# Splitting the loads of query and key rows, and a preparation buffer for the fourth weight's raw words, in a kernel of sparse attention and two MLPs

## The chip, the cores and the metric

The kernel runs on one core of a Trainium2 chip. The metric is the device time of one launch in microseconds (us), lower is better.

## The reference

Attention over 4 batches, 8 heads, 576 tokens and 64 elements per head is followed by two MLPs on 2304 tokens of width 512 with an inner width of 2048. The heads of the first half see the last 32 tokens, those of the second half every 32nd token before them.

```python
mask_local = (rel >= 0) & (rel < stride)
mask_strided = (rel >= 0) & (pos[None, :] % stride == pos[:, None] % stride)
scores = np.where(masks, scale * q @ k.T, -1e9);  attn = softmax(scores) @ v
h = x @ w_in;   g = s * relu(h) ** 2 + b;                     x = g @ w_out       # first MLP
h = x @ w_in;   g = where(h >= 1, h, where(h <= -1, 0, (h + 1) ** 2 / 4));  out = g @ w_out
```

The weights come as 64-bit floats.

## The kernel before

**Stages.** The tokens are cut into six units of 384. Attention is worked off in 21 tiles: three strided ones for each batch and nine local ones of 256 tokens; the text counts them in their order as tile 0, 1, 2 (strided, batch 0), 3, 4, 5 (local), 6, 7, 8 (strided, batch 1) and so on. A tile loads its rows, then PE makes scores, DVE takes the maximum (L611) and subtracts it (L628; in the first three tiles ACT's L622 does so in the exponential), ACT exponentiates (L631), DVE sums and inverts (L632 to L635), DVE or POOL normalizes (L636), PE transposes (the flip, L645), a copy brings the result to `pt` (L340 or L338), PE multiplies by the values (L661, L671), ACT copies the output to `xh` (L338) and DVE puts what the rounding lost into `xl` (L703). The first MLP (`hidden`, `output`) takes three matmuls for each product (high by high, high by low, low by high) and runs the segments unit 0, inner blocks 0 to 3; unit 1, blocks 0 to 3; unit 0, blocks 4 to 7; unit 1, blocks 4 to 7; then the other units. Unit 1 needs tiles 4 to 8. The second half of the first MLP and the whole of the second use a Strassen-like scheme with seven products, whose weights are made ahead by `prepare`, stored to DRAM from the ring `pp` (two buffers) by POOL (L401), and read back.

**Weights.** `decode` brings the words of one weight block into a buffer of the ring `raw` (three buffers, 512 KB each), ACT makes the high part of a 32-bit float (L356), DVE shifts and merges (L358, L360). `weights` splits that into a high and a low part (`w0h`, `w0l`; L338, L372). The first four blocks loaded are three of `w_ins` and one of `w_outs`; the fifth is of `w_ins` again.

**Order.** `Issue.order` is a list scheduler with costs and due times: it sets the order of all work on every engine when the program is built, and it also puts filler matmuls on the tile `warm_t` (`busy`, L576) where it expects PE to be idle in the first part. All loads go out on SP's queue in one order, save the small ones of tile 2 in batch 0, which ACT issues. The loads share eight completion semaphores (DMAHW0 to DMAHW7) in turn, so that a load is issued only when the one eight places before it has landed. `homes` names the tiles (0, 1, 3 to 7, 9, 11, 12) whose rows of queries and keys go to the space of later units' tokens (`xh5`, `xl5`, ..., printed without their number below). The two first tenants of the ring `pp` are `mask_t` and `warm_t`.

Of the kernel before, what the change touches and what calls it, by code (L numbers as in the profile page):

```python
# [12 lines left out]
I32 = mybir.dt.int32  # L13
# [6 lines left out]
DM, DFF = 512, 2048  # L20
# [10 lines left out]
KT = QT + STRIDE  # L31
# [11 lines left out]
HI_ACT, HOLD, NACC = 12, (0, 1, 3), 6  # L43
FILL, MOST, LEAST = 37.0, 5, (18.0, 2)
RAW, DT, KB, QV, SM, PT, PP, TB = 3, 2, 4, 3, 3, 2, 2, 3
BUFS = {"kb": KB, "qv": QV - 1, "qx": 1, "sm": SM - 1, "sx": 1, "pt": PT}


# [202 lines left out]
def sparse_attention_two_mlps(ctx: ExitStack, tc: tile.TileContext, loc, strd, w_ins, w_outs, fixed, out):  # L251
# [5 lines left out]
    sp = ctx.enter_context(tc.tile_pool(name="sp", bufs=2))  # L257
# [49 lines left out]
    def buf(pool, tag, shape, dtype=F32, bufs=1):  # L307
        ring = rings.setdefault((pool.name if hasattr(pool, "name") else id(pool), tag), Ring(bufs))
        ring.name = tag
        serial[0] += 1  # L310
        name = f"{tag}_{serial[0]}"
        return Buf(ring, lambda: pool.tile(shape, dtype, tag=tag, name=name, bufs=bufs))


    def act(n):
        return ("act", 0.15 + n * 0.00084, 0.1)
# [28 lines left out]
    decodes, prepared, pi_line, w_loads, w0_line, w1_line, p_line = [], [], [], [], [], [], []  # L345

    def decode(src, after=(), allocs=(), t=None, line=None, raw=None):
        raw = raw or buf(sp, "raw", [128, 2 * DM], I32, RAW)
        t = t or buf(sp, "dt", [128, DM], I32, DT)
        words = lambda i: raw.tile.rearrange("p (a b) -> p a b", b=2)[:, :, i]  # L350
        x = lambda: t.tile.bitcast(F32)
        load = op(lambda e: e.dma_start(out=raw.tile.bitcast(I64), in_=src), [dma(src.shape[0] * src.shape[1] * 8)],
                  writes=[raw], after=after, allocs=allocs, line=line)


        first = op(lambda e: e.activation(out=x(), in_=words(1).bitcast(F32), func=AF.Prelu, scale=2.0 ** -112, alpha=-2.0 ** 32),  # L356
                   [act(DM)], [raw], [t])
        op(lambda e: e.tensor_scalar(out=t.tile, in0=t.tile, scalar1=3, scalar2=None, op0=ALU.logical_shift_left),  # L358
           [dve2(DM, 0.0005)], (), [t])
        op(lambda e: e.scalar_tensor_tensor(out=t.tile, in0=words(0), scalar=29, in1=t.tile,  # L360
                                            op0=ALU.logical_shift_right, op1=ALU.bitwise_or), [dve2(DM)], [raw], [t])
        return t, x, first, load
# [84 lines left out]
    def attend(i, early):  # L447
        kind, b, d = tiles[i]
# [32 lines left out]
        QC, VC = 4 * 128, 4 * 128 + 2 * W  # L481
        if strided and d < 2:
            vb_ = room("vals")
            v4 = lambda: vb_.tile.rearrange("p (g n) -> p g n", g=2)
            if i in homes:
                both = home(homes[i][0])
                ks, qb_ = [both, both], both
                row = lambda: both.tile[:, 0:2 * VC].rearrange("p (j n) -> p j n", j=2)
                k4 = lambda j: row()[:, j, 0:QC].rearrange("p (h a n) -> p h a n", h=2, a=2)
                q4 = lambda j: row()[:, j, QC:VC].rearrange("p (h n) -> p h n", h=2)  # L490
                if i:
                    load(both, [(row, strd[b, 2 * d:2 * d + 2, :, 0:VC].rearrange("j p n -> p j n"))], 128 * 2 * VC * 4)
                else:
                    for j in range(2):
                        load(both, [(lambda j=j: row()[:, j], strd[b, 2 * d + j][:, 0:VC])], 128 * VC * 4)
            else:
                ks, qb_ = [room("wide") for _ in range(2)], room("wide")
                k4 = lambda j: ks[j].tile.rearrange("p (h a n) -> p h a n", h=2, a=2)
                q4 = lambda j: qb_.tile[:, 0:4 * W].rearrange("p (j h n) -> p j h n", j=2, h=2)[:, j]
                for j in range(2):  # L500
                    load(ks[j], [(lambda j=j: ks[j].tile, strd[b, 2 * d + j][:, 0:QC])], 128 * 2048)
                load(qb_, [(lambda: qb_.tile[:, 0:4 * W].rearrange("p (j n) -> p j n", j=2),
                            strd[b, 2 * d:2 * d + 2, :, QC:VC].rearrange("j p n -> p j n"))], 128 * 4 * W * 4)
# [37 lines left out]
        else:  # L541
            vs = [room("vals") for _ in range(2)]
            if i in homes:
                qs = ks = [home(tag) for tag in homes[i]]
                k4 = lambda pos: ks[pos].tile[:, 512:512 + 4 * KT].rearrange("p (a n) -> p a n", a=4)
                q4 = lambda pos: qs[pos].tile[:, 0:512].rearrange("p (a c n) -> p a c n", a=4, c=2)
            else:
                qs, ks = [room("wide") for _ in range(2)], [room("wide") for _ in range(2)]
# [3 lines left out]
            v4 = lambda pos: vs[pos].tile.rearrange("p (s h d) -> p s h d", s=2, h=4)  # L552
            for pos in range(2):
                if i in homes:
                    n = 512 + 4 * KT
                    load(qs[pos], [(lambda pos=pos, n=n: qs[pos].tile[:, 0:n], loc[2 * d + pos][:, 0:n])], 128 * n * 4)
                else:
                    load(qs[pos], [(lambda pos=pos: qs[pos].tile, loc[2 * d + pos][:, 0:512])], 128 * 2048)
                    load(ks[pos], [(lambda pos=pos: ks[pos].tile[:, 0:4 * KT], loc[2 * d + pos][:, 512:512 + 4 * KT])],
                         128 * 4 * KT * 4)  # L560
# [116 lines left out]
        for bank in range(2):  # L677
            cuts, bufs, n = [], [], 0
# [241 lines left out]
    n = NP  # L920
# [248 lines left out]
    for p in range(PAIRS):  # L1169
        a = len(plan.ops)  # L1170
# [118 lines left out]
```

## Time and profile before

| | us |
|---|---|
| median of 3 runs | 840.81 |
| the runs | 837.0 to 842.73 |
| the profiled execution | 843.28 |
| its span, first to last instruction | 840.7 |

PE is busy for 97% of the span, DVE for 75%, ACT for 63%, POOL for 11%; the DMA engines move 263 GB/s on average. The chain of work that ended last is 78% PE. The matmuls' ends are modelled, so a busy PE need not be one at its peak. In the first 70 us, where attention and the first weights are made, the engines wait for each other; behind that PE hardly stops.

### The profile page before, as it was taken

The page shows a single profiled execution, that of the slowest core. Times are in us where ns is not written, and L with a number is a line of the kernel's source. Part 1 is how long each engine was busy: PE and PEld are TensorE (multiplying, and loading weights), DVE is VectorE, ACT ScalarE, POOL GpSimd, SP SyncE. Part 2 cuts the span into 40 slices and gives each one's busy share as a digit, 9 for nine tenths or more (in the row PEclk, how much of TensorE's full clock was granted, in tenths as well). Part 3 has the DMA queues.
Part 4 walks back from the last instruction along what each step waited for, and adds up shares of the span by engine and source line. Part 5 has one row for each costly group of instructions (what it writes and reads, how often), then busy time and mean ns, then how long its engine had stood idle before and what let it go on. Part 6 is the DMA issues. An engine that isn't in the chain of part 4 may idle for free.

```text
span 840.7 us, 17752 instructions
## 1 busy us (share of the span) xinstructions
PE 817.7 (97%) x6308; PEld 793.1 (94%) x6312; DVE 628.7 (75%) x1333; ACT 528.3 (63%) x1122; POOL 91.5 (11%) x186
## 2 busy tenths in 40 slices
PE   7789999999999999999999999999999999999998
PEld 4579998999999999999988999999999999999998
DVE  3798638888776767878778977997576988466966
ACT  5467636565557666657576777865477854567653
POOL 1030003241221022130111000100000000000000
PEclk9999999999999999999999999999999999999999
DMA  8678285888777578899879899988987779888882
GB/s 255 215 226 287 96 259 189 288 274 275 252 264 275 184 272 277 308 315 335 296 253 319 262 372 311 331 252 268 304 255 252 253 250 283 294 253 252 249 267 95
DMA packets 107261, 221.15 MB, mean 263 GB/s; under 512 B 14118, under 2 KB 29606, under 8 KB 107174
## 3 DMA queue, kind: packets, MB, share of 16 engines
q1 hardware_dynamic: 95906, 182.89, 67.8%
q0 software_dynamic: 10240, 36.71, 11.4%
q8 instruction: 50, 0.82, 0.4%
q10 hardware_dynamic: 1028, 0.43, 0.2%
q14 instruction: 37, 0.30, 0.1%
HBM read 172.27 MB, written 47.71 MB: 262 GB/s over the span
## 4 chain that ended last, share of the span: by engine, by line
PE 78%; DMA 7%; issue 7%; DVE 5%; POOL 1%; ACT 1%; SPq 1%; ACTq 0%; POOLq 0%; DVEq 0%
PE acc L963 7%; PE acc L964 7%; PE acc L965 7%; PE h L720 6%; PE side L964 6%; PE side L963 6%; PE side L965 6%; PE h L721 6%; PE h L722 5%; PE h L964 3%; PE h L963 3%; PE h L965 3%; PE acc L720 3%; DMA dw<-pp 3%; PE acc L721 3%
## 5 line engine op out<-in xcount | busy, mean ns | idle before, releaser
L401 POOL DMA_DIRECT2D dw<-pp x80 | 54.9, 687 | 292.0 <-DVE pp L399 236.3
L720 PE MATMUL h<-xh,w0hx 128*128 128x384 f32 x192 | 65.5, 341 | 2.0 <-ACT w1hx L747 2.0
L720 PE MATMUL h<-xh,w0h 128*128 128x384 f32 x192 | 66.2, 345 | 0.8 <-issue 0.6
L721 PE MATMUL h<-xl,w0h 128*128 128x384 f32 x192 | 64.8, 337 | 0.7 <-DVE xl L703 0.7
L722 PE MATMUL h<-xh,w0lx 128*128 128x384 f32 x192 | 64.8, 338 | 0.0
L721 PE MATMUL h<-xl,w0hx 128*128 128x384 f32 x192 | 64.8, 337 | 0.0
L722 PE MATMUL h<-xh,w0l 128*128 128x384 f32 x192 | 64.6, 337 | 0.0
L747 ACT ACTIVATE t<-h 128x384 f32<-128x384 f32 x51 | 24.9, 488 | 31.0 <-PE h L722 30.8
L720 PEld LDWEIGHTS h<-xh,w0hx 128*128 128x128 f32 x192 | 36.2, 189 | 2.4 <-ACT w1hx L747 2.3
L720 PEld LDWEIGHTS h<-xh,w0h 128*128 128x128 f32 x192 | 36.3, 189 | 2.0 <-issue 0.7
L721 PEld LDWEIGHTS h<-xl,w0h 128*128 128x128 f32 x192 | 36.4, 189 | 1.0 <-DVE xl L703 1.0
L721 PEld LDWEIGHTS h<-xl,w0hx 128*128 128x128 f32 x192 | 36.3, 189 | 0.0
L722 PEld LDWEIGHTS h<-xh,w0lx 128*128 128x128 f32 x192 | 36.3, 189 | 0.0
L722 PEld LDWEIGHTS h<-xh,w0l 128*128 128x128 f32 x192 | 36.3, 189 | 0.0
L356 ACT ACTIVATE dt<-raw 128x512 f32<-128x512 f32 x42 | 27.7, 668 | 12.5 <-DMA raw<-in_w_outs 4.7
L338 ACT ACTIVATE gh<-w1h 128x384 fp32r<-128x384 f32 x48 | 24.6, 523 | 14.4 <-PE acc L965 6.3
L720 PE MATMUL acc<-gh,w1hx 128*128 128x384 f32 (+1 forms) x96 | 33.4, 348 | 0.0
L720 PE MATMUL acc<-gh,w1h 128*128 128x384 f32 (+1 forms) x96 | 33.4, 348 | 0.0
L1010 DVE TENSOR_TENSOR gl<-w1h,gh 128x384 fp32r<-128x384 f32 x48 | 26.2, 555 | 9.3 <-ACT gh L338 8.9
L399 DVE TENSOR_TENSOR pp<-dt,pp 128x512 fp32r<-128x512 f32 (+1 forms) x36 | 22.3, 619 | 14.0 <-ACT pp L338 13.9
L721 PE MATMUL acc<-gl,w1hx 128*128 128x384 f32 (+1 forms) x96 | 32.4, 338 | 0.0
L722 PE MATMUL acc<-gh,w1l 128*128 128x384 f32 (+1 forms) x96 | 32.4, 338 | 0.0
(585 smaller groups left out, 2813.0 us busy)
## 6 DMA issues: line engine op xcount, KB each, us to landing
dw<-pp POOLq DMA_DIRECT2D x60, 512.0 KB, 4.5
w0h<-dw SPq DMA_DIRECT2D x84, 256.0 KB
w0l<-dw SPq DMA_DIRECT2D x84, 256.0 KB
w0hx<-dw SPq DMA_DIRECT2D x84, 256.0 KB
w0lx<-dw SPq DMA_DIRECT2D x84, 256.0 KB
raw<-in_w_ins SPq DMA_DIRECT2D x32, 512.0 KB
raw<-in_w_outs SPq DMA_DIRECT2D x32, 512.0 KB
kb<-dw SPq DMA_DIRECT2D x56, 256.0 KB
```

The costliest lines, as they stand in the source:

```text
L338: e.activation(out=out, in_=in_, func=AF.Copy)
L356: first = op(lambda e: e.activation(out=x(), in_=words(1).bitcast(F32), func=AF.Prelu, scale=2.0 ** -112, alpha=-2.0 ** 32), [act(DM)], [r ...
L399: op(lambda e: e.tensor_tensor(out=y.tile[:, 0:nq, 1, :], in0=x(), in1=y.tile[:, 0:nq, 0, :].bitcast(F32), op=SUB), [dve2(256 * nq)], [b], ...
L401: op(lambda e: e.dma_start(out=dw[o][i][qs].rearrange("q p w n -> p q (w n)"), in_=y.tile[:, 0:nq].bitcast(F32).rearrange("p q w n -> p q ...
L720: e.matmul(out=acc, lhsT=wh, rhs=ah, start=first, stop=False)
L721: e.matmul(out=acc, lhsT=wh, rhs=al, start=False, stop=False)
L722: e.matmul(out=acc, lhsT=wl, rhs=ah, start=False, stop=last)
L747: op(lambda e: e.activation(out=c(t), in_=c(p), func=AF.Relu), [act(n)], [p], [t])
L963: e.matmul(out=dst, lhsT=wh, rhs=ah, start=opens and first, stop=False, skip_group_check=not opens)
L964: e.matmul(out=dst, lhsT=wh, rhs=al, start=False, stop=False, skip_group_check=not opens)
L965: e.matmul(out=dst, lhsT=wl, rhs=ah, start=False, stop=last, skip_group_check=not opens)
L1010: op(lambda e, g=g, hi=hi, lo=lo: e.tensor_tensor(out=lo.tile[:, 0:n], in0=g.tile, in1=hi.tile[:, 0:n].bitcast(F32), op=SUB), [dve2(n)], [ ...
```

## The change

A strided tile of `homes` after tile 0 loads its rows in four transfers (256, 126, 256 and 126 KB) in place of one of 764 KB. A local tile of `homes` loads each of its two row sets in two transfers (256 and 192 KB) in place of one of 448 KB. That is 15 and 8 transfers more. The raw words of the fourth weight block (the first of `w_outs`) go to a buffer of the ring `pp` in place of `raw`, so that the fifth block is the first that needs a `raw` buffer for the second time. The scheduler then orders everything anew.

```diff
--- before.py
+++ after.py
@@ -43,6 +43,7 @@
 HI_ACT, HOLD, NACC = 12, (0, 1, 3), 6
 FILL, MOST, LEAST = 37.0, 5, (18.0, 2)
 RAW, DT, KB, QV, SM, PT, PP, TB = 3, 2, 4, 3, 3, 2, 2, 3
+IN_PP = (3,)
 BUFS = {"kb": KB, "qv": QV - 1, "qx": 1, "sm": SM - 1, "sx": 1, "pt": PT}
 
 
@@ -345,7 +346,7 @@
     decodes, prepared, pi_line, w_loads, w0_line, w1_line, p_line = [], [], [], [], [], [], []
 
     def decode(src, after=(), allocs=(), t=None, line=None, raw=None):
-        raw = raw or buf(sp, "raw", [128, 2 * DM], I32, RAW)
+        raw = raw or (buf(sp, "pp", [128, 2 * DM], I32, PP) if len(w_loads) in IN_PP else buf(sp, "raw", [128, 2 * DM], I32, RAW))
         t = t or buf(sp, "dt", [128, DM], I32, DT)
         words = lambda i: raw.tile.rearrange("p (a b) -> p a b", b=2)[:, :, i]
         x = lambda: t.tile.bitcast(F32)
@@ -488,11 +489,9 @@
                 row = lambda: both.tile[:, 0:2 * VC].rearrange("p (j n) -> p j n", j=2)
                 k4 = lambda j: row()[:, j, 0:QC].rearrange("p (h a n) -> p h a n", h=2, a=2)
                 q4 = lambda j: row()[:, j, QC:VC].rearrange("p (h n) -> p h n", h=2)
-                if i:
-                    load(both, [(row, strd[b, 2 * d:2 * d + 2, :, 0:VC].rearrange("j p n -> p j n"))], 128 * 2 * VC * 4)
-                else:
-                    for j in range(2):
-                        load(both, [(lambda j=j: row()[:, j], strd[b, 2 * d + j][:, 0:VC])], 128 * VC * 4)
+                for j in range(2):
+                    load(both, [(lambda j=j, a=a, z=z: row()[:, j, a:z], strd[b, 2 * d + j][:, a:z])
+                                for a, z in (((0, VC),) if not i else ((0, QC), (QC, VC)))], 128 * VC * 4)
             else:
                 ks, qb_ = [room("wide") for _ in range(2)], room("wide")
                 k4 = lambda j: ks[j].tile.rearrange("p (h a n) -> p h a n", h=2, a=2)
@@ -552,8 +551,8 @@
             v4 = lambda pos: vs[pos].tile.rearrange("p (s h d) -> p s h d", s=2, h=4)
             for pos in range(2):
                 if i in homes:
-                    n = 512 + 4 * KT
-                    load(qs[pos], [(lambda pos=pos, n=n: qs[pos].tile[:, 0:n], loc[2 * d + pos][:, 0:n])], 128 * n * 4)
+                    load(qs[pos], [(lambda pos=pos, a=a, z=z: qs[pos].tile[:, a:z], loc[2 * d + pos][:, a:z])
+                                   for a, z in ((0, 512), (512, 512 + 4 * KT))], 128 * (512 + 4 * KT) * 4)
                 else:
                     load(qs[pos], [(lambda pos=pos: qs[pos].tile, loc[2 * d + pos][:, 0:512])], 128 * 2048)
                     load(ks[pos], [(lambda pos=pos: ks[pos].tile[:, 0:4 * KT], loc[2 * d + pos][:, 512:512 + 4 * KT])],
```

On SP's queue before, at the end of the loads of tiles 0 to 5: `raw` are the weights' words (0, 1, 2, 3 in order; two of `w_ins` and one of `w_outs` are seen), `xh`, `qv` and `k` belong to tile 6.

```order
L352 DMA raw_659<-in_w_ins 128x512 [waits DMAHW6_49]
L352 DMA raw_680<-in_w_ins 128x512 [waits DMAHW7_49]
L352 DMA raw_733<-in_w_outs 128x512 [waits DMAHW0_49,DMAHW1_49,DVE_49,Activation_49]
L467 DMA xh_127_746<-in_strd 128x2x764 [waits PE_49,Pool_49]
L467 DMA qv_776<-in_strd 54x2x256 [waits DMAHW2_49]
L467 DMA qv_776<-in_strd 54x2x256 [waits DMAHW3_49]
L467 DMA k_128_822<-in_strd 64x2x72 [waits DMAHW4_49,PE_49,Pool_49]
```

The same place after, and behind it the end of tile 7's loads (`xl`, `qx`) with the fifth weight (the last row).

```order
L353 DMA raw_684<-in_w_ins 128x512 [waits DMAHW7_49]
L353 DMA raw_737<-in_w_ins 128x512 [waits DMAHW0_49]
L353 DMA pp_750<-in_w_outs 128x512 [waits DMAHW1_49,DVE_49]
L468 DMA xh_127_760<-in_strd 128x512 [waits PE_49,DMAHW2_49,Activation_49,Pool_49]
L468 DMA xh_127_760<-in_strd 128x252 [waits DMAHW3_49]
```

```order
L468 DMA xl_140_862<-in_strd 128x512 [waits DMAHW5_49]
L468 DMA xl_140_862<-in_strd 128x252 [waits DMAHW6_49]
L468 DMA qx_901<-in_strd 54x2x256 [waits DMAHW7_49,PE_49]
L468 DMA qx_901<-in_strd 54x2x256 [waits DMAHW0_49]
L353 DMA raw_924<-in_w_ins 128x512 [waits DMAHW1_49,DVE_49,Activation_49]
```

The fourth weight no longer waits for ACT and for a `raw` buffer; the next wait of this kind is the fifth weight's, and ahead of it the values of tile 7 (`qx`) wait for PE.

On DVE before, around the normalization of tile 2 (`sx`, `dn_263`); `xl` rows are the outputs of tile 0.

```order
L633 TENSOR_SCALAR dn_263<-dn_263 128x8
L340 COPY pt_400<-h_399 128x512
L635 RECIPROCAL dn_263<-dn_263 128x8
L703 TENSOR_TENSOR xl_142<-side_305,xh_141 128x2x6x6
L703 TENSOR_TENSOR xl_140<-side_305,xh_139 128x2x6x12
L636 TENSOR_TENSOR sx_261<-sx_261,dn_263 128x512
L703 TENSOR_TENSOR xl_142<-side_306,xh_141 128x2x6x6
L703 TENSOR_TENSOR xl_140<-side_306,xh_139 128x2x6x12
```

POOL after, at the same place in the program: `sx` is tile 2 and `sm_352` tile 3, the copies after them are of tile 6's and tile 7's rows.

```order
L616 TENSOR_SCALAR mx_230<-mx_230 128x4
L616 TENSOR_SCALAR mx_267<-mx_267 128x4 x2
L635 TENSOR_TENSOR sx_266<-sx_266,dn_268 128x512
L635 TENSOR_TENSOR sm_352<-sm_352,dn_354 128x512
L632 TENSOR_SCALAR dn_632<-dn_632 128x8
L341 COPY k_128_839<-xh_127_760 64x2x18 x2
L341 COPY q_129_854<-xh_127_760 128x2x18
```

The normalizations of tiles 2 and 3 have moved from DVE to POOL. (On PE the values of tile 1 now stand ahead of the flip of tile 2, and the values of tile 3 ahead of the scores of tile 5.)

DVE before, from the maximum of tile 6 (`mx_862`) to its normalization (`sm_861`); `mx_932` is tile 7.

```order
L611 TENSOR_REDUCE mx_862<-side_859 128x4
L611 TENSOR_REDUCE mx_862<-side_860 128x4
L628 TENSOR_TENSOR sm_861<-side_859,mx_862 128x256
L628 TENSOR_TENSOR sm_861<-side_860,mx_862 128x256
L372 TENSOR_TENSOR w1l_735<-dt_849,w1h_734 128x512
L632 TENSOR_REDUCE dn_863<-sm_861 128x8
L753 TENSOR_TENSOR t_901<-t_901 128x384
L611 TENSOR_REDUCE mx_932<-side_929 128x4
L635 RECIPROCAL dn_863<-dn_863 128x8
L611 TENSOR_REDUCE mx_932<-side_930 128x4
L636 TENSOR_TENSOR sm_861<-sm_861,dn_863 128x512
```

The same stretch after (tile 6 is `mx_878` and `sm_877`, tile 7 is `mx_951`).

```order
L373 TENSOR_TENSOR w1l_752<-dt_849,w1h_751 128x512
L627 TENSOR_TENSOR sm_877<-side_875,mx_878 128x256
L627 TENSOR_TENSOR sm_877<-side_876,mx_878 128x256
L758 TENSOR_TENSOR gl_845<-t_843,gh_844 128x384
L752 TENSOR_TENSOR t_907<-t_907 128x384
L631 TENSOR_REDUCE dn_879<-sm_877 128x8
L610 TENSOR_REDUCE mx_951<-side_949 128x4
L610 TENSOR_REDUCE mx_951<-side_948 128x4
L634 RECIPROCAL dn_879<-dn_879 128x8
L758 TENSOR_TENSOR gl_909<-t_907,gh_908 128x384
L635 TENSOR_TENSOR sm_877<-sm_877,dn_879 128x512
```

Two splits of a hidden block (`gl`), which POOL had before, stand on DVE now. Behind this stretch, up to tile 7's normalization, one `dt` row (the shift) is added. From the start up to the last `xl` row of tile 8, DVE has 130 rows before and 135 after: four copies `pt`, one merge `dt`, one shift `dt`, one small `mx` row and three `gl` more; two normalizations, two squares `t` and one `w0l` fewer. On PE order and rows are the same from about row 1826 of 5294 on, but for tile numbers.

## Rows read from the trace of the kernel before

**Rows 1.** Page, part 1: busy us, share of the span, instructions of each engine.

```profile
PE 817.7 (97%) x6308; PEld 793.1 (94%) x6312; DVE 628.7 (75%) x1333; ACT 528.3 (63%) x1122; POOL 91.5 (11%) x186
```

**Rows 2.** Windows: stretch, busy us (and count) by engine, granted clock, DMA share, GB/s.

```profile
30.00:36.00 6.00, 3.49 (x74) 2.82 (x76) 4.00 (x13) 0.73 (x3) 0.07 (x1) 0.84 0.18 68
41.00:58.00 17.00, 13.45 (x216) 11.83 (x215) 15.13 (x35) 10.58 (x23) 7.60 (x13) 1.00 0.81 246
58.00:70.00 12.00, 11.22 (x132) 9.74 (x131) 11.02 (x30) 8.18 (x23) 0.60 (x1) 0.86 0.73 233
70.00:400.00 330.00, 328.22 (x2894) 318.03 (x2893) 243.80 (x550) 203.30 (x418) 65.84 (x130) 1.00 0.76 259
400.00:460.00 60.00, 56.23 (x311) 55.50 (x310) 47.60 (x100) 39.22 (x83) 11.04 (x16) 0.97 0.84 288
```

**Rows 3.** Waits of PE in the whole span: us in total, times, longest.

```profile
PE h L720 <- ACT w1hx L747: 2.0, 1, 2.0
...
PE acc L963 <- DMA sx<-dw: 1.8, 1, 1.8
```

**Rows 4.** Waits of SP's DMA queue from 0 to 60 us: us, times, longest.

```profile
SPq L352 <- DVE dt L360: 16.0, 2, 10.4
```

**Rows 5.** Timeline of SP's queue: start, us, queue, line, transfer, count.

```profile
24.06 1.43 SPq L352 DMA_DIRECT2D raw<-in_w_ins  x2
36.58 0.33 SPq L352 DMA_DIRECT2D raw<-in_w_outs  x1
43.57 0.69 SPq L467 DMA_DIRECT2D qx<-in_strd  x2
44.36 0.36 SPq L352 DMA_DIRECT2D raw<-in_w_ins  x1
```

**Rows 6.** Chain of work that ended last, 0 to 90 us: start, us, what.

```profile
3.86 5.66 DMA xl<-in_strd
9.54 0.28 ACTq L467
10.98 0.24 ACT sm L622
```

**Rows 7.** Timeline of DVE, POOL and ACT: start, us, what, idle before it and releaser.

```profile
10.10 0.24 DVE L617 TENSOR_SCALAR mx<-mx 128x4 f32<-128x4 f32 x1
28.39 0.63 ACT L631 ACTIVATE sm<-sm 128x512 f32<-128x512 f32 x1 [0.50 <-DVE sm L628]
42.62 1.21 POOL L340 COPY k<-xh 64x36 f32<-64x36 f32 x2 [12.55 <-DMA xh<-in_strd]
45.82 0.43 DVE L358 TENSOR_SCALAR dt<-dt 128x512 int32<-128x512 int32 x1
50.09 0.69 DVE L632 TENSOR_REDUCE dn<-sm 128x8 f32<-128x512 f32 x1 [0.98 <-ACT sm L631]
67.72 0.55 DVE L759 TENSOR_TENSOR gl<-t,gh 128x384 fp32r<-128x384 f32 x1
```

**Rows 8.** Timeline of PE: start, us, what, idle before it and releaser.

```profile
23.34 0.63 PE L645 MATMUL h<-fix_t,sx 128*128 128x128 f32 x4 [1.57 <-DVE sx L636]
24.26 0.69 PE L661 MATMUL side<-pt,w0lx 54*64 54x54 f32 x32
33.32 0.37 PE L671 MATMUL side<-pt,w1lx 64*64 64x32 f32 x11 [1.92 <-issue]
41.07 0.42 PE L720 MATMUL h<-xh,w0h 128*128 128x384 f32 x1
57.71 0.91 PE L645 MATMUL h<-fix_t,sm 128*128 128x128 f32 x4 [2.95 <-DVE sm L636]
69.08 0.44 PE L721 MATMUL h<-xl,w0h 128*128 128x384 f32 x1 [0.70 <-DVE xl L703]
```

**Rows 9.** DMA from 0 to 30 us (total), and from 30 to 31 us by queue.

```profile
DMA packets 4208, 8.02 MB, mean 267 GB/s; under 512 B 1158, under 2 KB 1862, under 8 KB 4205
q8 instruction: 1, 0.02, 7.1%
```

## The prediction

> **What bounds the kernel now.** I read the page first: PE is busy for 97% of the span [rows 1], so the time can only move by what PE loses. The windows say where that is. From 70 to 400 us PE loses 330 − 328.22 = 1.8 us, from 400 to 460 us 3.8 us, and from 41 to 70 us 29 − 13.45 − 11.22 = 4.3 us [rows 2]. Ahead of 41.07 us, when the first matmul of the MLP starts [rows 8], PE does attention and filler only, so this start S is the largest single loss. The timeline of PE then names the places [rows 8]: tile 7's flip waits 2.95 us for DVE's normalization, tile 2's flip 1.57 us, and for 1.92 us of "issue" PE stands still in the middle of tile 3's values though nothing is awaited. The waits add two stalls behind 400 us, 2.0 and 1.8 us [rows 3]. What the change aims at is on SP: the fourth weight's load waits 10.4 us for DVE [rows 4]. SP issues the third weight at about 25 us and the fourth only at 36.58 us [rows 5], and from 30 to 36 us the DMA engines are busy for 0.18 of the time only [rows 2].
>
> **The wait that is removed.** The fourth weight now needs a buffer that `mask_t` left by about 7 us, so SP goes on at about 25.5 us with the rows of tiles 6 and 7. Who waited for these? POOL's copies of tile 6's keys did, 12.55 us, until 42.62 us [rows 7]. But PE, in its fixed order, was busy with the first hidden blocks by then: of the 17 − 13.45 = 3.55 us that it loses from 41 to 58 us [rows 2], 2.95 are tile 7's flip [rows 8]. So the removed wait hid behind PE's own work, and by itself it is worth 0 to the other 0.6 us; I take 0. And the stall has a successor: tile 7's values (`qx`) may be loaded only when tile 5's values have been used by PE, and the fifth weight queues behind them. Before, that was at 43.57 us, the fifth weight at 44.36 us [rows 5]; it follows S, so weights five and on come only about as much earlier as S does.
>
> **The transfers.** 23 more transfers, 9 of them ahead of the first weights. A transfer costs SP about 0.35 to 0.7 us [rows 5], so the first weight's load is issued up to 9 × 0.4 = 3.6 us later, if SP and not the data is the limit. In the first 30 us 8.02 MB came at 267 GB/s [rows 9], so the data is nearer to being the limit, and the same bytes are moved. The weights have some 5 us between landing and use, which hides it; with that cover gone it would cost up to 3.6 us at S. The Trainium skill ("DMA: Bandwidth & Descriptors", "Rules for kernel authors") speaks against this edit: it wants at least 1 MiB in a transfer and small ones merged, and its fit gives each a fixed 2.0 us; by it, paid one after another, 23 more would be an estimated 46 us. The row on the first 30 us does not bear that out, since transfers in flight overlap there. The one gain I can see is on ACT: it issues tile 2's small loads itself, and the shared semaphores made one of them wait for all 764 KB of tile 1 (5.66 us, to 9.54 us); its first exponentials began at 10.98 us [rows 6], though the maximum was ready at 10.10 + 0.24 = 10.34 us [rows 7]. With pieces, the wait can end earlier: 0 to 0.64 us, I take 0.6.
>
> **The new order, up to S.** Tile 2's normalization goes to POOL, and PE does tile 1's values ahead of tile 2's flip. The flip's 1.57 us of idle time [rows 8] is filled by 0.69 us of values at least: 0.69 to 1.57, I take 1.2. On ACT the exponential of tile 4 (0.63 us) stood ahead of the copies of tile 2's output [rows 7], which free the PSUM buffers that tile 3's values want; after, it stands behind them: 0 to 0.63, I take 0.6. The fillers are 64 before and 63 after: 0. PE's standstill of 1.92 us [rows 8] may go or repeat. In the microsecond before it the queue of instructions had one packet of 16 KB, which took 7.1% of 16 engines, 1.1 us, on full engines [rows 9]; so I read it as PE waiting for its own instructions. The new order has as many instructions in less time, and DMA now stays busy beyond 32 us: between −1.92 (gone) and +1.92 (a second one), I take 0. Sum: S is 0.6 + 1.2 + 0.6 = 2.4 us earlier, 38.7 us, with ends at 36.4 (everything gained, standstill gone) and 42.5 (only 0.69 gained, a second standstill, and half a us of late weights).
>
> **The new order, behind S.** From 41 to 58 us DVE is busy for 15.13 of 17 us, and PE waits for it at 57.71 us for 2.95 us [rows 2, 8]. After, DVE has two splits `gl` and a shift more between tile 6's maximum and tile 7's normalization: 2 × 0.55 + 0.43 = 1.5 us [rows 7]. Some of that fits into DVE's idle 0.98 us there [rows 7]. So 0.5 to 1.5 us later; the upper bound is the whole of what DVE has more up to tile 8's last `xl`: 4 copies of 0.68 (as one merge), 3 `gl`, one shift, one merge and a small row, 5.8 us, against two normalizations and a `w0l` of about 0.69 and two squares of 0.56, 3.2 us; 2.6 us. I take 1.2, nearest to the stretch that PE waits for. PE cannot overtake this: the first block of unit 1 waits for tile 8's `xl` as before (0.70 us) [rows 8].
>
> **Behind 70 us** PE's rows are the same from 1826 on, ACT's and DVE's differ in places. The two stalls of 2.0 and 1.8 us there [rows 3] may go or double: 0, with ±3.8.
>
> **The sum.** −2.4 + 1.2 = −1.2 us. Against the profiled execution's 843.28 us that is 842.1; the median of the runs shown is 840.81, 2.5 below it, so I forecast 840.81 − 1.2 = 839.6 us.
>
> **Rivals.**
> The gain stays (a): tile 7's flip finds its normalization ready, because DVE also starts earlier. Then S is 4.7 earlier, the 2.95 us go, and so does the low clock behind them: 58 to 70 us ran at a granted 0.86 [rows 2], that is 28% of the stretch at the lower of the two levels, 1.2 of 2.4 GHz, some 1.7 us lost. Together 9.3 us, 831.5. For it: DVE has idle time ahead of 41 us. Against it: its list is longer, and all of this must come together.
> The change does not do what it says (b): the wait only moves to `qx`, DVE eats the earlier start: 840.8 us.
> Instructions come late (c), the one on the other side: with the DMA engines busy from 25 to 41 us, each fetch of PE's instructions in the dense part (some three more between 30 and 46 us) costs the 1.92 us that one cost at 31.4 us: +5.8 − 1.2 = 4.6 us, 845.4. It decides if more than one fetch stalls. For it: the place of the standstill, at the end of a full stretch. Against it: only one of the earlier fetches shows it. The Trainium skill ("DMA: Bandwidth & Descriptors", "Queues, rings and completion order") says that an engine goes round its queue rows packet by packet, which would bound such a delay; no row here shows the rounds.
> Small transfers lower the rate (d): if the 9 extra ones hold SP for 3.6 us and DVE's 2.6 us come on top, S and the rest lose 6.2, 847; with the late stalls doubled (3.8) it passes 850. For it: the count of transfers. Against it: 267 GB/s with several in flight [rows 9]. The Trainium skill's rule on small transfers, named above, lies on this side.
>
> **How the numbers follow.** Forecast, 837 to 841: 0.45. (b), 840 to 842: 0.20. (a): 0.13, of which 0.10 below 832.4. (c): 0.14. (d): 0.08, of which 0.06 above 849.2. 1% is 8.4 us, about what a measurement of this kernel can tell from no change; so faster 0.10, same 0.84, slower 0.06. The range takes in most of (a) short of its full size and all of (c): 833.5 to 847, with about 0.2 left out.
>
> **What would show it.** SP issues the fourth weight by 28 us and waits for PE at `qx` near 41 us; ACT's first exponential near 10.3 us; the first `h` matmul near 38.7 us; tile 7's flip waits for DVE for 3 to 4 us; the last wait for tile 8's `xl` ends near 68 us; behind that, waits of PE under 6 us in all. It is wrong if the first `h` matmul starts later than 41 us (c or d), or if tile 7's flip does not wait (a).

## The result and the profile after

The changed kernel takes 851.79 us (median of 4 runs, 849.49 to 853.91); the kernel before, run beside it, 841.77 us. The ratio is 1.0108, with an interval of 1.0067 to 1.0148: slower by about 1%. The profiled execution of the changed kernel took 852.1 us, with a span of 850.0. (One profile below, that of `s1_after`, was taken in an execution of 865.99 us, 2.2% above the fastest of that kernel, and is not read.)

The page's first part, as [rows 1]: PE has hardly more work, and the span is 9.3 us longer, so the time went into waits and into matmuls at the lower clock.

```profile
PE 821.2 (97%) x6307; PEld 795.2 (94%) x6311; DVE 633.2 (74%) x1335; ACT 525.5 (62%) x1116; POOL 94.8 (11%) x190
```

The windows of [rows 2] again:

```profile
30.00:36.00 6.00, 5.36 (x171) 4.53 (x175) 4.75 (x14) 2.16 (x6) 0.00 (x0) 1.00 1.01 344
41.00:58.00 17.00, 14.42 (x213) 11.98 (x213) 14.97 (x34) 11.01 (x25) 1.61 (x7) 0.94 0.63 196
58.00:70.00 12.00, 9.91 (x125) 8.82 (x126) 11.08 (x27) 6.34 (x17) 1.39 (x2) 0.86 0.55 169
70.00:400.00 330.00, 324.39 (x2850) 312.78 (x2849) 239.35 (x541) 196.42 (x409) 71.24 (x134) 0.99 0.75 254
400.00:460.00 60.00, 59.98 (x343) 59.66 (x341) 46.71 (x97) 40.20 (x82) 10.23 (x15) 1.00 0.86 291
```

The hole in the transfers from 30 to 36 us is closed (DMA share 1.01 instead of 0.18). From 58 to 70 us PE loses 2.1 us where it lost 0.8, and from 70 to 400 us 5.6 where it lost 1.8. From 400 to 460 us it loses nothing any more, where the kernel before lost 3.8; but this is in part the border of the window, since waits of 0.64 and 1.81 us follow right behind it:

```profile
460.62 0.44 PE L962 MATMUL acc<-gh,kb 128*128 128x384 f32 x1 [0.64 <-ACT gh L339]
...
465.58 0.44 PE L963 MATMUL acc<-pt,sx 128*128 128x384 f32 x1 [1.81 <-DVE pt L1009]
```

Waits of PE, as [rows 3]. The one of 2.0 us that stood there is gone; the one of 1.8 us, which stood at 458.69 us, has the last of these in its place:

```profile
PE h L644 <- DVE sm L635: 4.5, 2, 3.9
...
PE h L719 <- ACT t L746: 3.0, 1, 3.0
PE side L575 <- DVE xl L702: 3.0, 2, 1.8
...
PE acc L963 <- DVE pt L1009: 1.8, 1, 1.8
```

SP's queue, as [rows 5]: the first weight, the fourth (into `pp`), tile 7's values (`qx`), the fifth weight.

```profile
24.39 0.43 SPq L353 DMA_DIRECT2D raw<-in_w_ins  x1
...
28.47 0.35 SPq L353 DMA_DIRECT2D pp<-in_w_outs  x1
...
45.38 0.69 SPq L468 DMA_DIRECT2D qx<-in_strd  x2
46.18 0.35 SPq L353 DMA_DIRECT2D raw<-in_w_ins  x1
```

The fourth weight is asked for 8.1 us earlier. But `qx` now waits from 40.2 us (the end of the row before it) to 45.38, and the fifth weight comes 1.8 us later than before. The first weight comes 4.8 us later, behind more transfers; in the kernel before it was asked for here:

```profile
19.62 0.37 SPq L352 DMA_DIRECT2D raw<-in_w_ins  x1
```

ACT's first exponential, as in [rows 6]: 0.21 us earlier.

```profile
10.77 0.31 ACT L621 ACTIVATE sm<-acc,mx 128x64 f32<-128x64 f32 x1 [0.70 <-DMA w1hx<-in_strd]
```

PE's timeline, as [rows 8]: the standstill in tile 3's values, the first `h`, the flips of tiles 5, 6 and 7, tile 8's `xl`, and a place near 386 us.

```profile
38.57 0.30 PE L670 MATMUL side<-pt,w1hx 64*64 64x32 f32 x2 [1.68 <-issue]
39.92 0.69 PE L719 MATMUL h<-xh,w0h 128*128 128x384 f32 x1 [1.05 <-ACT w0h L339]
40.40 0.52 PE L720 MATMUL h<-xl,w0h 128*128 128x384 f32 x1
...
42.96 0.71 PE L644 MATMUL h<-fix_t,sx 128*128 128x128 f32 x4 [0.22 <-issue]
...
54.76 0.66 PE L644 MATMUL h<-fix_t,sm 128*128 128x128 f32 x4 [0.55 <-DVE sm L635]
...
60.09 1.01 PE L644 MATMUL h<-fix_t,sm 128*128 128x128 f32 x4 [3.91 <-DVE sm L635]
...
72.28 0.44 PE L720 MATMUL h<-xl,w0h 128*128 128x384 f32 x1 [1.18 <-DVE xl L702]
...
385.88 0.69 PE L719 MATMUL h<-xh,w0hx 128*128 128x384 f32 x1 [2.99 <-ACT t L746]
386.37 0.52 PE L720 MATMUL h<-xl,w0hx 128*128 128x384 f32 x1
```

The first `h` comes 1.15 us earlier than before, with the clock at its lower level behind the two waits (0.52 us a matmul instead of 0.34), and ahead of tile 5's flip; in the kernel before that flip, at 40.66 us, stood ahead of the first `h`. Tile 7's flip waits 3.91 us instead of 2.95.

The wait of 1.05 us ahead of the first `h` is for the first weight's high part, `w0h`. ACT after, and ACT before:

```profile
38.90 0.45 ACT L339 ACTIVATE xh<-side 128x128 fp32r<-128x128 f32 x2 [1.53 <-PE side L670]
39.23 0.63 ACT L339 ACTIVATE w0h<-dt 128x512 fp32r<-128x512 f32 x1
...
37.16 0.62 ACT L338 ACTIVATE w0h<-dt 128x512 fp32r<-128x512 f32 x1
```

In the new order `w0h` stands on ACT behind the copy of tile 3's output, and that copy waits for PE's values, in which PE stands still for 1.68 us. So the first `h` cannot come sooner than a copy and `w0h` after tile 3's values.

To see where the 9.3 us arise I number the matmuls of 384 and more columns, fillers left out, with the first `h` as number 0. Their order on PE is nearly the same in all kernels, so the k-th can be compared. Stretches in us, from the start of one to the start of another:

| stretch | before | after | difference |
|---|---|---|---|
| start to the first `h` | 41.07 | 39.92 | −1.15 |
| first `h` to the 84th (behind tile 8's `xl`) | 28.98 | 33.35 | +4.37 |
| 84th to the 1630th | 303.33 | 302.99 | −0.34 |
| 1630th to the 1742nd (after: 376 to 402 us) | 20.06 | 26.15 | +6.09 |
| 1742nd to the 2326th | 108.01 | 108.35 | +0.34 |
| 2326th to the last | 335.45 | 335.38 | −0.07 |

So two places make the loss, the stretch behind the first `h` and one near 385 us. The stretch that has the stalls behind 400 us (1742nd to 2326th) takes as long as before.

### The profile page after: what moved, and what is told of

Same layout as the page of the kernel before. It is cut to its first block, busy times and chain, and to the rows that moved or that the text cites. A ratio compares the mean times of both kernels' runs of the same rounds, so it can differ in the third digit from the quotient of the medians.

```text
span 850.0 us, 17814 instructions
## 1 busy us (share of the span) xinstructions
PE 821.2 (97%) x6307; PEld 795.2 (94%) x6311; DVE 633.2 (74%) x1335; ACT 525.5 (62%) x1116; POOL 94.8 (11%) x190
## 4 chain that ended last, share of the span: by engine, by line
PE 71%; issue 13%; DMA 6%; DVE 4%; POOL 3%; SPq 2%; ACT 2%; ACTq 0%; POOLq 0%; DVEq 0%
PE acc L963 7%; PE acc L964 6%; PE acc L962 6%; PE side L963 5%; PE side L964 5%; PE side L962 5%; PE h L719 4%; PE h L720 4%; PE h L721 4%; PE acc L719 3%; PE h L963 3%; PE h L962 3%; PE h L964 3%; PE acc L721 3%; PE acc L720 3%
## 5 line engine op out<-in xcount | busy, mean ns | idle before, releaser
L721 PE MATMUL acc<-gh,w1lx 128*128 128x384 f32 (+1 forms) x96 | 32.5, 338 | 0.0
L720 PE MATMUL acc<-gl,w1h 128*128 128x384 f32 (+1 forms) x96 | 32.4, 337 | 0.0
L758 DVE TENSOR_TENSOR gl<-t,gh 128x384 fp32r<-128x384 f32 x41 | 22.7, 554 | 12.2 <-ACT gh L339 12.2
```

Of the source, the lines that this page charges most:

```text
L720: e.matmul(out=acc, lhsT=wh, rhs=al, start=False, stop=False)
L721: e.matmul(out=acc, lhsT=wl, rhs=ah, start=False, stop=last)
L758: op(lambda e: e.tensor_tensor(out=c(gl), in0=c(t), in1=c(gh).bitcast(F32), op=SUB), [pool(n)] + [dve2(n)], [t, gh], [gl])
```

## Experiments

**Which part of the edit.** The planner counts a cost for each transfer, so splitting the loads changes the order of all engines; the buffer alone leaves every row of every engine where it was. This allows the parts to be taken one by one. `e1`: the changed kernel with the raw words back in the `raw` ring.

```diff
-IN_PP = (3,)
+IN_PP = ()
```

> The split of the loads alone; the fourth weight's words stay in the ring raw. The scheduler's order on PE, DVE, ACT and POOL is then that of the changed kernel, row for row. Three theories. Order: the loss sits in the new order, so this takes 848 to 853 us, as the changed kernel. Transfers: the small transfers cost, 848 to 853 too. Buffer: the loss comes with the buffer in pp, so this takes 838 to 843. SP waits again for DVE at the fourth weight, 8 to 11 us.

`e2`: the kernel before with the buffer alone.

```diff
+IN_PP = (3,)
...
-        raw = raw or buf(sp, "raw", [128, 2 * DM], I32, RAW)
+        raw = raw or (buf(sp, "pp", [128, 2 * DM], I32, PP) if len(w_loads) in IN_PP else buf(sp, "raw", [128, 2 * DM], I32, RAW))
```

> The buffer alone; loads as before. The scheduler's order on the engines is then that of the kernel before, row for row, but SP's wait for the fourth weight is gone. Order: 838 to 843 us. Transfers: 838 to 843. Buffer: 848 to 853. If the wait of SP did bound the start, the first matmul of the MLP comes 1 us or more ahead of 41.1 us; I expect it within 0.7 us of that.

`e3`: the order of the kernel before, with the split loads and the buffer. The planner is told of the whole load, and the pieces are issued in its place.

```diff
-        def load(y, parts, size, queue="sp", line=a_line):
+        def load(y, parts, size, queue="sp", line=a_line, issued=None):
             ways = [dma(size, len(parts), queue)]
+            parts = issued or parts
...
```

> Both edits, but every engine's order is that of the kernel before: the scheduler is told the old costs and the old ring, only what is issued is new. Order: 838 to 843 us, the first wait for tile 8's output ends within 1 us of 69 us. Transfers or buffer: 848 to 853, with it 72 us or later.

`e4`: the other way round, the order of the changed kernel with whole loads and the `raw` ring, by the same `issued`.

> Neither edit, but every engine's order is that of the changed kernel: the scheduler is told the new costs and the new ring, while whole transfers are issued and the fourth weight goes to raw. Order: 848 to 853 us, the first wait for tile 8's output ends at 72 us or later, and PE waits for ACT for about 3 us near 385 us. Transfers or buffer: 838 to 843, 70 us or earlier, no such wait.

| kernel | order | loads | ratio to before, interval | first `h` to 84th | 1630th to 1742nd |
|---|---|---|---|---|---|
| before | old | whole | 1 | 28.98 | 20.06 |
| e2, buffer alone | old | whole | 1.0009, 0.9982 to 1.0035 | 28.46 | 19.57 |
| e3 | old | split | 1.0025, 1.0005 to 1.0045 | 28.45 | 19.57 |
| after | new | split | 1.0108, 1.0067 to 1.0148 | 33.35 | 26.15 |
| e1, split alone | new | split | 1.0056, 1.0030 to 1.0083 | 33.85 | 23.21 |
| e4 | new | whole | 1.0083, 1.0049 to 1.0117 | 34.82 | 24.73 |

The loss goes with the order, whatever the loads are: 33.4 to 34.8 us against 28.5 to 29.0 behind the first `h`, and 23 to 26 against 20 us near 385. (By the whole time alone `e1` and `e3` could not be told apart; the stretches tell them.) With the old order held, the split loads and the buffer cost 0.05 to 0.45%. In `e2` SP issues the fourth weight at 29.18 us instead of 36.58, and the first `h` comes at 41.66 instead of 41.07 us: the wait that the change removes was worth nothing.

**The early place: three rows more on DVE?** My first theory was that DVE's longer list sets the pace. `e7` gives the first three splits (`gl`) of the changed kernel back to POOL, `e8` gives those of the kernel before to DVE; no other row moves.

```diff
         for o in self.order():
+            if o in FIRST[:3]:
+                o.eng = "pool"
...
```

> The changed kernel; only the first three hidden units' splits (gl, 128x384) go back from the vector engine, where they took 0.51 to 0.56 us each at 48.6, 51.0 and 53.6 us, to the gpsimd engine, where the kernel before had them. Nothing else in any engine's list moves. Theory 1 (behind the first h the vector engine's list sets the pace, and the new order has put three rows more on it): the wait of 3.91 us ahead of tile 7's flip falls by some 1.4 us to 2.5, tile 8's parts come 1 to 1.6 us earlier, and from there to the end the kernel stands 1 to 2 us below the changed one (ratio to before 1.009 instead of 1.011). Rival (the loss in that stretch is the engine clock of 0.5 behind the standstill at 38.6 us and the late first weight): the flip's wait stays at 3.5 to 4 us or only turns into another one, and the time stays within 0.5 us of the changed kernel's.

> The kernel before; only the first three hidden units' splits (gl, 128x384), which took 1.02 to 1.46 us each on the gpsimd engine, go to the vector engine at the same places of the order. The mirror of the run before it. Theory 1: the wait ahead of tile 7's flip grows from 2.95 us to about 4, tile 8's parts come 1 to 1.6 us later, the end 1 to 2 us (ratio 1.001 to 1.002). Rival: no difference beyond 0.5 us, since the vector engine has room there in the old order.

`e8` bears the theory out in part only: from the first `h` to the 84th it takes 30.76 us, 1.8 more than before, but tile 7's flip waits 2.69 us, less than the 2.95 before and not the 4 that were expected, and the ratio (1.0015, 0.9990 to 1.0040) cannot be told from 1. `e7` speaks against it: 1.0103 (1.0073 to 1.0133), 35.74 us, and the flip waits as long as ever. PE, then DVE and POOL in `e7`:

```profile
61.87 1.11 PE L650 MATMUL h<-fix_t,sm 128*128 128x128 f32 x4 [3.91 <-DVE sm L641]
...
55.21 1.27 DVE L641 TENSOR_TENSOR sm<-sm,dn 128x512 f32<-128x512 f32 x1
...
54.92 1.01 POOL L764 TENSOR_TENSOR gl<-t,gh 128x384 fp32r<-128x384 f32 x1
```

The splits were not what the flip waits for. And while POOL works on a split, tile 6's product on DVE takes 1.27 us instead of 0.68. The changed kernel has the same between tile 6's flip and tile 7's. DVE and POOL there:

```profile
58.19 1.25 DVE L359 TENSOR_SCALAR dt<-dt 128x512 int32<-128x512 int32 x1
59.36 0.68 DVE L635 TENSOR_TENSOR sm<-sm,dn 128x512 f32<-128x512 f32 x1
...
57.89 1.26 POOL L373 TENSOR_TENSOR w0l<-dt,w0h 128x512 fp32r<-128x512 f32 x1
```

A `dt` row that takes 0.42 to 0.43 us elsewhere [rows 7] takes 1.25 while POOL works on `w0l`, and tile 7's product stands behind it. `e13` gives this one `w0l` to DVE, behind tile 8's subtractions (rows 201 and 293 of the planner's list); `e14` also puts the `dt` row behind tile 7's product (rows 212 and 279). `moved` is a few lines that put the first of a pair behind the second in the planner's finished order.

```diff
-        for o in self.order():
+        for o in moved(self.order()):
...
+    next(o for o in rows if o.n == 201).eng = "dve"
+    for a, b in ((201, 293), (212, 279),):
```

> The changed kernel; one row moves: the low half of a weight (w0l), which gpsimd computed at 57.89 us in 1.26 us, goes to the vector engine behind the subtraction of tile 8's maxima. In the changed kernel a row of the vector engine that takes 0.42 us elsewhere (dt on int32, 128x512) took 1.25 us at 58.19, just as long as that gpsimd row ran, and it stands ahead of the product that tile 7's flip waits for. Theory 3 (the two engines get in each other's way and the wait is lengthened by it): the dt row takes 0.42 us again, the flip's wait falls from 3.91 to about 3.1 us, tile 8's parts come up to 0.8 us earlier, the time falls by 0.3 to 1 us. Rival (the long row is a coincidence, the row waited for its operand): it stays at 1.2 us and the flip's wait at 3.9.

> As the run before it, and the dt row itself goes behind the product (sm times dn) of tile 7, so that between the row sums and the product only the maxima and the reciprocal are left on the vector engine. Theory 3: the flip's wait falls by 1.2 us against the changed kernel, to about 2.7; from flip to flip 4.1 us instead of 5.33 (the kernel before: 4.24); the time falls by 0.7 to 1.5 us. Rival (what follows the flip is bound by the weights, not by the flip): the first weight parts behind it come later by what was saved, the flip's wait falls but the time stays.

`e13`, DVE (the `dt` row and tile 7's product) and PE (the flips of tiles 6 and 7):

```profile
59.69 0.38 DVE L359 TENSOR_SCALAR dt<-dt 128x512 int32<-128x512 int32 x1
59.98 0.68 DVE L635 TENSOR_TENSOR sm<-sm,dn 128x512 f32<-128x512 f32 x1
...
56.26 0.66 PE L644 MATMUL h<-fix_t,sm 128*128 128x128 f32 x4 [0.55 <-DVE sm L635]
60.72 1.12 PE L644 MATMUL h<-fix_t,sm 128*128 128x128 f32 x4 [3.03 <-DVE sm L635]
```

`e14`, PE's flips of tiles 6 and 7, and tile 6's in the kernel before:

```profile
56.79 0.66 PE L644 MATMUL h<-fix_t,sm 128*128 128x128 f32 x4 [0.54 <-DVE sm L635]
61.08 0.66 PE L644 MATMUL h<-fix_t,sm 128*128 128x128 f32 x4 [2.86 <-DVE sm L635]
...
53.47 0.60 PE L645 MATMUL h<-fix_t,sm 128*128 128x128 f32 x4
```

The mechanism is shown: 0.38 us again, and from flip to flip 4.46 and 4.29 us instead of 5.33 (4.24 before: 53.47 to 57.71). The time is another matter: 1.0065 (1.0034 to 1.0096) and 1.0076 (1.0043 to 1.0110), not to be told from the changed kernel; from the first `h` to the 84th 34.51 and 32.53 us, against 33.35. Some 1 us of the 4.4 is found in this chain; that it comes back in the whole time is not shown.

**The late place.** Near 385 us PE waits 2.99 us for ACT. ACT keeps its order and stands before a write into the `pp` ring, which must wait for a store of POOL to land. In the changed kernel, rows of SP, POOL and ACT:

```profile
358.66 0.86 SPq L353 DMA_DIRECT2D raw<-in_w_outs  x2
361.40 0.33 SPq L884 DMA_DIRECT2D kb<-dw  x1
...
358.97 0.73 POOL L402 DMA_DIRECT2D dw<-pp  x1 [3.22 <-ACT gh L339]
...
367.84 0.42 ACT L339 ACTIVATE pp<-sm 128x256 fp32r<-128x256 f32 x1 [6.99 <-DMA dw<-pp]
...
384.82 0.63 ACT L339 ACTIVATE pp<-qv 128x512 fp32r<-128x512 f32 x1 [3.37 <-DMA dw<-pp]
```

The same place in the kernel before:

```profile
356.48 0.38 SPq L352 DMA_DIRECT2D raw<-in_w_outs  x1
359.22 0.32 SPq L885 DMA_DIRECT2D kb<-dw  x1
359.64 1.08 SPq L352 DMA_DIRECT2D raw<-in_w_outs  x1
...
356.92 1.57 POOL L401 DMA_DIRECT2D dw<-pp  x2 [3.79 <-ACT pp L338]
...
363.87 0.42 ACT L338 ACTIVATE pp<-sm 128x256 fp32r<-128x256 f32 x1 [4.22 <-DMA dw<-pp]
```

From the store's issue to the write that waits for it: 8.9 us after, 6.95 before. In the new order the two loads of raw weights, 512 KB each, stand side by side around the store. The same holds for `e1` and `e4`, where this store takes 8.7 and 9.0 us to land; with the loads apart it takes 6.3 in `e2`. `e11` moves the second behind `kb`, as it was; `e12` also moves one ACT row (this write, behind `pt<-w1l`) and two small POOL copies (behind a store).

```diff
+    for a, b in ((1884, 1964),):                              e11
...
+    for a, b in ((1963, 1814), (1802, 1944), (1884, 1964),):  e12
```

> The changed kernel; only one row of SyncE's list moves: of the two raw loads of weights that stand side by side at 358.66 us, the second goes behind the load of a stored part (kb) that follows them, as the kernel before had it. Theory 2 (the late loss of some 6 us starts with a store from the preparations' ring at 358.97 us that took 8.9 us to land, where in the kernel before the one at 356.92 took 6.95, because two raw loads were issued ahead of it instead of one): that store lands about 2 us sooner, ScalarE's wait of 6.99 us at 367.8 falls to about 5, TensorE's wait of 2.99 us near 385 falls below 1.5 or is gone, the low clock behind it too, and the time falls by 3 to 6 us. Rival (the landing has nothing to do with that row, or the stall comes from how the rows lie on ScalarE and gpsimd): ScalarE's wait stays at 6.5 to 7 us and the time within 1 us of the changed kernel's.

> The changed kernel with three rows moved near 360 us, as the kernel before had them: the row of SyncE as in the run before; on ScalarE the blocked write into the preparations' ring (128x256, which waited 6.99 us at 367.8) goes behind the copy pt<-w1l; on gpsimd two small copies (0.5 us) go behind a store. Theory 2a (the late stall is the local order of these three rows): TensorE's wait near 385 (2.99 us) and the low clock behind it are gone, and the time falls by 5 to 6 us, to a ratio to before of about 1.004. Theory 2b (only the transfers matter): the same as the run that moves the one row of SyncE. Rival (the stall is set by how far the preparations have got against TensorE, and local rows only shift it): a wait of 2 us or more shows within the next 60 us, as the kernel before has one of 2.00 at 428.85, and the time falls by 2 us or less.

`e11`, rows of SP, POOL and ACT:

```profile
364.12 0.38 SPq L353 DMA_DIRECT2D raw<-in_w_outs  x1
366.86 0.32 SPq L884 DMA_DIRECT2D kb<-dw  x1
367.27 0.54 SPq L353 DMA_DIRECT2D raw<-in_w_outs  x1
...
363.70 0.73 POOL L402 DMA_DIRECT2D dw<-pp  x1 [3.24 <-ACT gh L339]
...
369.88 0.42 ACT L339 ACTIVATE pp<-sm 128x256 fp32r<-128x256 f32 x1 [3.57 <-DMA dw<-pp]
...
383.06 0.63 ACT L339 ACTIVATE pp<-qv 128x512 fp32r<-128x512 f32 x1 [1.61 <-DMA dw<-pp]
```

One row of one queue: from the store to the write 6.2 us, ACT's wait 3.57, PE's wait gone, and from the 1630th to the 1742nd 20.35 us (`e12`: 19.57) instead of 26.15. The five other kernels that keep the new order there (`e1`, `e4`, `e7`, `e13`, `e14`) all have the wait, of 2.4 to 3.2 us. The times: `e11` 849.8 us, 1.0072 (1.0046 to 1.0097); `e12` 845.81 us, 1.0024 (1.0001 to 1.0046), whose interval lies below that of the changed kernel. In `e11` some of the gain is given back in its profile: from the 1742nd to the 2326th it takes 110.80 us (after 108.35, `e12` 107.05). That the other two rows of `e12` prevent this is not shown: `e15` below has them and takes 109.35, and the kernels in the old order, with the same rows there, take 108.0 to 110.8.

`e15` has the five moved rows of `e12` and `e14` together.

> The two rows of the run before and the three rows moved near 360 us together. If the losses are separate places that add, the late part gives some 5 to 6 us as it did alone (845.8 against 851.8) and the early part 0.7 to 1.5 more: a ratio to before of 1.000 to 1.002. If the early gain is swallowed on the way (the vector engine reaches the next stall earlier and waits there), the ratio is that of the late rows alone, 1.0024.

1.0045 (1.0012 to 1.0078): no gain beyond that of `e12` shows, though the interval would hide one microsecond. No kernel here is measurably faster than the one before.

**The draw or the edit?** The planner adds a random term to each due time. `s1`, `s2` and `s3` start it with another number, for the kernel before and the changed one.

```diff
-SEED, JITTER = 19, 0.3
+SEED, JITTER = 1, 0.3
```

> The kernel before with another start of the order's random term (1 instead of 19); transfers and buffers as they were. If a draw of the order costs as much as the change did, this kernel differs from the kernel before by 0.3% or more in one direction or the other, most likely slower, as 19 is one draw that was kept. If the draw hardly matters, within 0.3%.

> The changed kernel with start 1 instead of 19. If the edit itself brings the loss (smaller costs per transfer make the order send rows ahead that delay the first weights, whatever the draw), it is 0.5 to 1.2% above its partner with start 1. If the loss is the draw's, it is within 0.5% of its partner, on either side.

> The kernel before with start 2. As with start 1: a draw's own effect shows as a distance of 0.3% or more from the kernel before.

> The changed kernel with start 2. The edit's own effect would show as 0.5 to 1.2% above its partner with start 2, in the same direction as with start 1; the draw's as a difference of another size or sign.

> The kernel before with start 3 of the order's random term. As a draw alone: anywhere from 1.000 to 1.011 of the kernel before; tile 8's parts within 2 us of the kernel before's 70 us.

> The changed kernel with start 3. If the early loss is the edit's, tile 8's parts come 2.5 us or more behind its partner's, for the third time; if it is the draw's, at 1.5 us or less. The late part is expected to differ by any sign; so the whole is 0 to 1.2% above its partner in the first case.

| start | without the edit | with it | 84th matmul at, without and with |
|---|---|---|---|
| 19 | 1 | 1.0108, 1.0067 to 1.0148 | 70.06, 73.27 |
| 1 | 1.0105, 1.0070 to 1.0141 | 1.0118, 1.0031 to 1.0205 | 70.44, not read |
| 2 | 1.0011, 0.9979 to 1.0043 | 1.0133, 1.0079 to 1.0186 | 71.83, 74.74 |
| 3 | 0.9992, 0.9967 to 1.0017 | 1.0078, 1.0045 to 1.0110 | 67.32, 73.10 |

From the first `h` to the 84th, starts 2 and 3 take 28.64 and 28.49 us without the edit and 33.50 and 33.43 with it: an early loss of 4.4 to 4.9 us comes with the edit in all three draws that were read. Its make-up differs: in start 3 with the edit no flip there waits more than 0.9 us. The stall near 385 us hardly comes with it: from the 1630th to the 1742nd it is 21.39 us, with a wait of 1.33 us at that place, and 20.01. The profiles of start 2 do not account for the whole difference: the two profiled executions (851.35 and 853.27 us) lie 1.9 us apart, the medians 10.8. And a draw by itself can cost as much as the change did: start 1 without the edit is at 1.0105, with a wait of 5.0 us for ACT's `pt` in a place of its own. The pair of start 1 shows no difference, but its interval with the edit, from three runs, is wide; the other three show 0.9 to 1.2%.

## Why the prediction was wrong, point by point

The direction failed: 1.2 us less were forecast, some 10 us more were measured, and the range ended at 847. Of the two signs that were to show it wrong neither came: the first `h` began before 41 us, and tile 7's flip waited. What did come out otherwise is tile 8's `xl`, at 72.28 us in place of 68.

**The removed wait: right.** It was to be worth 0 and to reappear at `qx`. `e2` shows the 0; the stall at `qx` ends at 45.38 us, 1.8 us later than its old place, and delays the fifth weight.

**The transfers: little cost, but not none.** Old order with split loads: 0.05 to 0.45%, 0.4 to 3.8 us, where the sum had 0; the buffer alone shows 0.09%, not to be told from nothing. The first weight was to be asked for up to 3.6 us later; it was 4.8 us in the changed kernel and 3.3 in `e3` (22.92 us). That is not what PE waits for at the first `h`: `e4`, with whole loads, asks for it at 19.66 us, and PE waits 1.38 us for `w0h` all the same. The rule on small transfers of the Trainium skill ("DMA: Bandwidth & Descriptors", "Rules for kernel authors") that the prediction weighed, and its estimate of 46 us for 23 more, do not decide here: `e3` stands at most 3.8 us above the kernel before. Rival (d), at 847 and beyond, came nearest to the time, but by luck: `e4`, with whole loads, lost as much. On ACT the pieces gave 0.21 us, not 0.6.

**Up to the first `h`: half of the 2.4 us came, and it measured the wrong thing.** The changed profile shows 1.15. PE was through with tile 3's values at 38.87 us, close to the forecast of 38.7; then it waited 1.05 us for `w0h`, for whose place in ACT's list the prediction had no term. (The upper end for S, 42.5, should by its own parts have been 42.8; nothing hangs on it.) Over the kernels with the new order (up to there the same rows but for loads and buffers) the first `h` begins between 39.06 and 43.26 us, the middle of nine at 40.12; in the old order at 41.07, 41.66, 41.91 and 42.97. The new order gains the time partly by putting the first `h` ahead of tile 5's flip. That work then stands behind it: the first twelve matmuls take 5.80 us instead of 3.46, at the low clock for a part, behind a standstill of 1.68 us and the wait of 1.05. I had taken the first `h` as the mark of progress, and a mark that the order itself can shift is none.

**Behind the first `h`: the step that failed.** It was priced at 1.2 us, with bounds of 0.5 and 2.6, by counting DVE's extra rows. It measured 4.37 us, and 4.4 to 5.8 in the kernels of the tables with the new order, each against its partner in the old one (for `e1` and `e4`, the kernel before). By stretches: +2.3 us up to the 12th matmul (the clock, a filler and the shifted flip), −1.5 up to the 36th, +2.8 up to the 48th (1.5 us more of waiting at the flips of tiles 6 and 7, and attention work that stood elsewhere before), −1.1 up to the 72nd, +1.8 up to the 84th (tile 8's `xl`, 1.18 us of waiting instead of 0.70, again attention work, and the clock behind the wait). Of these only tile 7's flip had been expected; its wait of 3 to 4 us was right, and the reason was not: `e7` shows that the extra splits did not make it. A `dt` row held up by POOL did make 0.9 us of it (`e13`). The two profiles divide the 4.4 us: PE is idle for 6.1 us of the stretch instead of 4.3, the 84 matmuls take 18.3 instead of 16.8, at the low clock behind the waits, a filler takes 0.65, and the attention work 8.3 instead of 7.9. DVE's added rows, the only thing that was priced, do not explain it: the splits alone cost 1.8 us in the old order (`e8`), but taking them off DVE in the new one won nothing (`e7`). Why the other waits came stays open.

**Behind 70 us: a term sized from the wrong end.** "0, with ±3.8" took the two old stalls and let them go or double. The first went, the second came again at the same row (1.81 us at 465.58, now for DVE's `pt`), and their stretch changed by 0.3 us only; but a new loss of 6.1 us came at a place that had lost next to nothing: a write into a full ring, one load that moved in SP's list, and a wait that ends in the low clock. PE's rows are the same there, and I had taken that as a sign that little could happen; the cause lay in SP's rows, of which the prediction says nothing.

**Rival (c)**, the one on the slower side, had the sign and about the size of the early part (+4.6 us against −1.15 + 4.37 = +3.2) by the wrong mechanism, which is luck: in the changed profile the standstill appears once, as before.

## What to carry to other kernels

Where a planner sets the order, a change to a load's cost is a change to every engine's order: compare all queues down to the end, and measure edit and order apart (old order with the new loads, new order with the old ones) before anything is said of the edit. Measure progress at a mark that no order can move work past, here the 84th matmul and not the first. And an engine that keeps its order and writes into a small ring can be as late as the slowest store of that ring, so look at which loads stand beside the store in the other queues.

## What the runs showed of the hardware

**POOL can hold DVE up.** `dt`, 128x512 on int32, takes 0.42 us alone and 1.25 us while a POOL row with two inputs runs; the product `sm` 1.27 us instead of 0.68 in `e7`. With POOL's row gone the first was 0.38 us (`e13`). The Trainium skill ("SBUF — State Buffer", "SBUF: two separate sides") says that the two share a pair of ports, held by one of them for a whole instruction. The rows agree: the two long rows end 0.29 and 0.55 us behind the end of POOL's rows (59.15 us, and 55.93 in `e7`), near the 0.42 and 0.68 us that they take alone, as if they had only begun then. That DVE holds POOL up in turn is not shown here.

**The landing of a store depends on its neighbours.** From the issue of the store to the write that it blocks 8.9 us passed with two loads of 512 KB side by side around it, and 6.2 us in `e11`, where one of them had moved. By its landing it is 8.7 to 9.0 us in three kernels with the loads side by side and 6.2 to 7.5 in four with them apart (before, `e2`, `e11`, `e12`).

**A wait costs more than its length.** Behind the wait of 2.99 us fifteen matmuls run at 0.52 us with starts 0.32 us apart, until 391 us, against 0.34 and 0.17 behind them: some 2.2 us on top. The granted clock from 360 to 400 us is 0.91, which is a fifth of that window at the lower of the two levels, 1.2 of 2.4 GHz.

**The same rows, a different start.** Kernels whose rows are the same up to the first `h` reach it between 39.06 and 43.26 us. The standstill of PE in tile 3's values, in which nothing is awaited, was 0.29 us in `e1`, 1.68 in the changed kernel and 2.5 in `e11`. A difference of a few us in that stretch between two single profiles says nothing by itself.
